# PSUM in eight tiles of one bank instead of four of two, reads of one bank each, and a new order of steps, in a fused attention and mixture-of-experts kernel

## The chip, the cores and the metric

The kernel runs on one core of a Trainium2 chip. The metric is the device time of one execution in microseconds; before the change it is 699.67 us, the median of three runs (698.33 to 700.05).

## What is computed

Linear attention feeds a mixture of four attention experts. Per batch (8) and head (8), with 576 positions and 64 channels:

```
phi(x) = concat(exp(p), exp(-p)),  p = x @ w_phi - max|x @ w_phi|        # 2 x 128 features
num = phi(q) @ (phi(k)^T v);  den = phi(q) @ sum(phi(k)) + 1e-6;  attn = num / den
```

The heads side by side give x (8 x 576 x 512). Each expert e projects x to q, k and v (512 to 64), takes causal softmax attention over the 576 positions and projects back to 512. The two experts with the largest gate logits (x @ w_gate) are kept per position, weighted with the softmax over their two logits, and added. The layout of inputs and outputs is prepared outside the timed program. All is in float32; the projections of x split each operand into a high and a low part (float32r) and take three products.

## The kernel before, in words

The work is cut into pairs of heads, 32 in all, p = 0 to 31, and into batches b = 0 to 7, each with two groups g of two experts. Generators describe the streams, and every `yield` is one step on one engine:

- `stream_k`: projects k of a pair on PE; `center` reduces its absolute maximum on DVE (L353) and subtracts it into the tile ek (L356); two exponentials follow on ACT. `stream_kv` multiplies by v and copies the result to kv.
- `stream_q`: projects q; `evac_u` copies the result out; `phi_q` takes the maximum over partitions on POOL (L438), subtracts on DVE (L447), and takes two exponentials on ACT. `stream_n` multiplies by kv, `divide` (with `normed`, L379 to L387) divides, `turn_x` transposes on PE (L393) and `evac_x` writes the high part xh and the low part xl.
- `stream_b`, per batch: `proj_t` projects q and k of a group in two pieces of 256 and 320 positions; `evac_q` and `evac_k` write high parts (qh on ACT at L171, kkh at L169 or L180) and low parts (ql at L522, kkl at L165) on DVE. `proj_v` projects v and the gate logits (vs; lg at L543). `scores` multiplies in four steps, `soft` adds the causal mask (L571), copies the scores to st, and keeps the running maximum in top (L588). `post` takes the maximum over partitions on POOL, subtracts (L673), exponentiates and multiplies with v on PE; `norm_y` divides, `turn_y` transposes, `evac_y` writes yh and yl, and `project_out` and `evac_o` make the output tile ot, which SP stores.

Every matmul writes to PSUM, which holds 128 partitions by eight banks of 512 floats. The kernel has four PSUM tiles of two banks each, all named ps_c in the profile. A step takes either one bank of a tile (`proj_t`, `proj_v`, `stream_kv`, the transpositions, `project_out`) or both (`stream_k`, `stream_q`, `stream_n`, `scores`, `post`); after the latter, one instruction on DVE or ACT reads both banks at once. The tile framework adds the semaphores, from which tile an instruction reads or writes.

The order of all steps is fixed in advance by the string PICKS: each pair of letters names the stream that moves on, and the bank that its step takes, or whether ACT or DVE does the copy. `take` hands out banks by their number, (tile, half):

```python
banks = [(i // 2, i % 2 + k) for k in range(st.n)]
keys = [('c', *x) for x in banks]
```

`in_order` then makes every engine keep the order in which the steps were recorded. `keep_warm` fills PE's first microseconds with small bf16 matmuls without a use.

Of the kernel before, what the change touches and what calls it, by code (L numbers as in the profile page):

```python
# [8 lines left out]
F32 = mybir.dt.float32  # L9
# [3 lines left out]
ALU = mybir.AluOpType  # L13
# [23 lines left out]
BANKS = 4  # L37
# [12 lines left out]
    "EACACACABABAAAAABAAAAAAAAAAAFCCAFEMADADAEGCAMAMAECNIFEBAAAPAAAOIAAAAAAFENIBAAAOAAANIAAAAFGFEEAOINAHAAAMIGAAAOAAAAACAAAEA"  # L50
    "ECEGBAMAPIJBHAQIGAPIOAMADAFEOIJAFCCAOAGIKGOAMIEAGACAEAEEPIOAMAECBAJBQIMAQIGAPIDAOGJAOHPAOIAAPAAAFEOIKCEAOINIOAEAMIEGNAOI"
    "JBDAMAPIMAEEGIJAFCMANICAMBAAPALALIMAJGOAPIAAGIMALIMIDAMIGAECMIDAFADEDAAAOINAIGGAOINIFACANIMHIAMCMAJEOIFIFANADANIMILIDAEA"
    "BAMIDCNAFAEGNALAMAOIMBPAIECAQAFINAMIKAMIEGHALIECGALAKIEEBAMALADAMAIGNIAAOIFIJAMIJAIAIAICFIBALIDAIDMAKADAJILENALFLIMAGACA"
    "NAFIJAMIMIJAKIDGJIGAFADEAAKIECJAHAMAMILIKIJAJIFAECBAEGJIKAEELAKAICLABAFIDAIDLIIGLAHHKILADAKIKIDAKIJAIIDEAAFGKIIALIKICAIA"
    "HAHHFIJIHGKAJIIIDAHCDAKIKIJIGAKIJIIAJIIAFDCAIIDEFIDGAAJIGAKIJIHCJIJIJIDAHDDAKIHAHEKIKIHGKILIHAMAKILAHCLAHAHGLIKAMILIMILA"
    "LIHHOAKIMALIHEOANIKAKIMIHFKILALIKAIEIAKALAKIIBIGKAHADCMAJIKAJIDEAAKIFAKIIICAKIEGIAIIFAECBALAJIKAGGLIJIIAKAIIJIIAIIDAEAII"
    "ECBAMAEEMAEAKIIABALAKCDANIKDIGIIMANAKALIIALILIIAHAKIJAHEHCMALIKEMILAKFMIFGCALIMIMALAMILIJIKADAFAKIDEAAKIHGJAGCJALIJIKIJI"
    "KAHAHAHAKIJIHBJINADAIIJADAHELILINAIALFMINILGHHLIMALIMAIALIIIHADCLIDAAAIAIIFELIIAKILICAIILIEGFAIAIIEEBALAGAIILAKIIALAMIKI"
    "IGMIKIDADAEELIDCMAFACAMIJILBFALELIJAHFLAMALIJAKIHGKAKIHHKAKIDCAAKAKIEAKIGELAMIKIKADABAHGDALIHHMAMIKIHAHAMAHCHEOIPAMIKANI"
    "HGOINAHAHCKALIHDMIPANILAMAMINIHAQAMILIMAMIHBQALAPILIMILAJANAMIJEJFMALIMAJGHADCNAKIKIKADAAAKIFHMIKILIKICAEEFAJIEABALAGGLA"  # L60
    "KIJAKAJIDAEEEABANALILIICJAIDJIMADANIIENIMAKIJANAIFNALELGMAJINAMAIHNADAKAJIDCAAKALIFFLIMIJANILACALIJGFAKIJIDAHEDAKIKIHAHC"
# [33 lines left out]
class Plan:  # L95
# [16 lines left out]
    def release(self, tag, t):  # L112
        self.free.add(t[0][1:])

    def take(self, st, i):
        banks = [(i // 2, i % 2 + k) for k in range(st.n)]
        assert all(x in self.free for x in banks)
        self.free -= set(banks)
        keys = [('c', *x) for x in banks]
        return (keys[0], self.both[i // 2][:, i % 2, :]) if st.n == 1 else (*keys, self.both[i // 2])  # L120

    def loop(self):
        for i, x in zip(PICKS[::2], PICKS[1::2]):
# [20 lines left out]
def tile_linear_attn_moe(ctx, tc, qt, kt, v, wts, out):  # L144
# [5 lines left out]
    plan.both = [pp.tile([128, 2, 512], F32, name=f"ps_c{i}") for i in range(BANKS)]  # L150
    plan.free = {(i, h) for i in range(BANKS) for h in range(2)}
    for t in plan.both:
        nc.vector.memset(t[:, :, NJ * V1 - 1:NJ * V1], 0.0)
# [171 lines left out]
    def stream_k():  # L325
        for p in range(NPAIRS):
            x, need = k_in[p % IB], [(f'k_in{p % IB}', n) for n in range(3)] + ['wphi']
            ready = lambda: ('load_k', p) in done and ('w', 0) in done
            for us in (slice(0, 8), slice(8, 9)):
                k0, k1, pp_ = yield Step('PE', need, 'c', ready, tiling=(64, 128), n=2)  # L330
                for n in range(4) if us.start == 0 else (4,):
                    for h, pk in enumerate((k0, k1)):
                        r = slice(64 * h, 64 * h + 64)
                        half_mm(pp_[:, h, 128 * (n % 4):128 * (n % 4) + 128], x[r, 128 * n:128 * n + 128], wf[r, 0:128], 128, pk, need)
                plan.spawn(center(p, us, (k0, k1), pp_))
            done.add(('proj_k', p))
            i = p % EKB
            ek, e0k, e1k = ek2[i], f'ek{i}0', f'ek{i}1'
            yield Step('ACT', [e1k], pred=lambda: all(('center', p, t) in done for t in (0, 8)))
            act(1152, ek[:, 0], ek[:, 1], [e0k], [e1k], AF.Exp)  # L340
            yield Step('ACT')
            act(1152, ek[:, 1], ek[:, 1], [e1k], [], AF.Exp, scale=-1.0)
            done.add(('phi_k', p))

    def center(p, us, pk, pp_):
        m, mk, e1 = pmax[p % 2], ('pmax', p % 2, us.start), ek2[p % EKB][:, 1, us, :]
        if us.start == 0:
            parts = [(slice(0, 128), 8, pp_.rearrange("p h (u f) -> p (h u) f", f=128))]
        else:
            parts = [(slice(64 * h, 64 * h + 64), 1, pp_[64 * h:64 * h + 64, h:h + 1, 0:128]) for h in range(2)]  # L350
        yield Step('DVE', list(pk), hot=True)
        for r, n, src in parts:
# [468 lines left out]
```

## Time and profile before

| | |
|---|---|
| median of 3 runs | 699.67 us |
| profiled execution | 699.21 us, span 697.4 us |
| busy: PE, DVE, ACT, POOL | 615.6, 508.4, 368.0, 200.6 us |
| mean granted TensorE clock | 0.977 |
| DMA | 43.45 MB, mean 62 GB/s |

How to read what follows: "L162" is a line of the kernel, "ps_c<-xh,qk" means that the instruction writes ps_c and reads xh and qk, "128x256" is partitions by elements per partition. "x6" counts instructions. In brackets stands the idle time of the engine ahead of an instruction, and what released it. PE is TensorE's matmuls, PEld its weight loads, DVE VectorE, ACT ScalarE, POOL GpSimd, SP the engine that issues DMAs.

### The profile page before, as it was taken

The page shows a single profiled execution, that of the slowest core. Times are in us where ns is not written, and L with a number is a line of the kernel's source. Part 1 is how long each engine was busy: PE and PEld are TensorE (multiplying, and loading weights), DVE is VectorE, ACT ScalarE, POOL GpSimd, SP SyncE. Part 2 cuts the span into 40 slices and gives each one's busy share as a digit, 9 for nine tenths or more (in the row PEclk, how much of TensorE's full clock was granted, in tenths as well). Part 3 has the DMA queues.
Part 4 walks back from the last instruction along what each step waited for, and adds up shares of the span by engine and source line. Part 5 has one row for each costly group of instructions (what it writes and reads, how often), then busy time and mean ns, then how long its engine had stood idle before and what let it go on. Part 6 is the DMA issues. An engine that isn't in the chain of part 4 may idle for free. (4 is left out here: it accounts for less than half of the span.)

```text
span 697.4 us, 22344 instructions
## 1 busy us (share of the span) xinstructions
PE 615.6 (88%) x9880; PEld 553.8 (79%) x9880; DVE 508.4 (73%) x1127; ACT 368.0 (53%) x561; POOL 200.6 (29%) x79
## 2 busy tenths in 40 slices
PE   8999998899888998988888888899988988987885
PEld 7888896888777897887778778788888777876774
DVE  6899788886696766898478767768576786555572
ACT  4988536566373544774146645454246455344442
POOL 5345306342242112542034332411060241120220
PEclk9999999999999999999999999899999999999999
DMA  7555213122131201423023031222112000010012
GB/s 199 130 152 153 63 39 90 40 58 56 39 108 37 75 20 38 127 74 75 3 70 91 19 82 31 57 72 75 30 46 90 18 22 0 3 53 18 1 53 85
DMA packets 60272, 43.45 MB, mean 62 GB/s; under 512 B 44688, under 2 KB 47248, under 8 KB 60176
## 3 DMA queue, kind: packets, MB, share of 16 engines
q1 hardware_dynamic: 60176, 42.03, 21.4%
q8 instruction: 77, 1.26, 0.7%
q14 instruction: 19, 0.16, 0.1%
HBM read 32.58 MB, written 9.44 MB: 60 GB/s over the span
## 5 line engine op out<-in xcount | busy, mean ns | idle before, releaser
L438 POOL PARTITION_ALL_REDUCE mx<-u x32 | 130.0, 4081 | 193.6 <-ACT u L169 193.5
L162 PE MATMUL ps_c<-xh,qk 128*128 128x320 f32 (+1 forms) x512 | 110.4, 302 | 10.2 <-DVE ql L522 6.5
L162 PEld LDWEIGHTS ps_c<-xh,qk 128*128 128x128 f32 x512 | 84.4, 190 | 14.3 <-DVE ql L522 7.8
L368 PE MATMUL ps_c<-v_in,ek 128*64 128x65 f32 x2560 | 87.6, 231 | 4.2 <-issue 0.9
L368 PEld LDWEIGHTS ps_c<-v_in,ek 128*64 128x64 f32 x2560 | 83.5, 146 | 8.4 <-DVE xl L165 1.3
L171 ACT ACTIVATE ek<-ek 128x1152 f32<-128x1152 f32 x64 | 74.6, 1166 | 22.8 <-DVE ek L356 22.3
L438 POOL PARTITION_ALL_REDUCE tops<-top x15 | 57.5, 3832 | 73.2 <-DVE top L588 73.2
L162 PE MATMUL ps_c<-xl,qk 128*128 128x256 f32 (+1 forms) x256 | 76.0, 297 | 0.0
L673 DVE TENSOR_TENSOR st<-st,tops 128x1152 f32<-128x1152 f32 (+4 forms) x75 | 68.8, 937 | 1.2 <-POOL tops L438 0.7
L171 ACT ACTIVATE st<-st 128x1152 f32<-128x1152 f32 (+3 forms) x60 | 51.4, 870 | 33.7 <-DVE st L673 32.7
L162 PE MATMUL ps_c<-vg,xh 128*128 128x260 f32 (+1 forms) x320 | 61.2, 290 | 8.2 <-DVE lg L543 5.0
L162 PE MATMUL ps_c<-yh,wo 128*128 128x256 f32 (+1 forms) x256 | 56.1, 311 | 13.5 <-ACT ot L169 3.7
L169 ACT COPY st<-ps_c 128x1024 f32<-128x1024 f32 (+1 forms) x58 | 47.2, 833 | 36.0 <-PE ps_c L560 17.8
L368 PE MATMUL ps_c<-kv,mx 128*64 128x65 f32 x1152 | 63.1, 227 | 2.9 <-ACT kv L169 1.9
L353 DVE TENSOR_REDUCE pmax<-ps_c 64x1 f32<-64x128 f32 (+1 forms) x96 | 56.3, 596 | 11.7 <-PE ps_c L323 10.3
L368 PE MATMUL ps_c<-kv,u 128*64 128x65 f32 x1152 | 60.2, 224 | 0.0
L356 DVE TENSOR_TENSOR ek<-ps_c,pmax 64x128 f32<-64x128 f32 (+1 forms) x96 | 56.3, 597 | 1.8
L162 PEld LDWEIGHTS ps_c<-vg,xh 128*128 128x128 f32 (+1 forms) x320 | 47.6, 178 | 11.6 <-DVE lg L543 6.7
L162 PEld LDWEIGHTS ps_c<-yh,wo 128*128 128x128 f32 x256 | 40.4, 189 | 20.2 <-ACT ot L169 5.6
L368 PEld LDWEIGHTS ps_c<-kv,mx 128*64 128x64 f32 x1152 | 48.2, 140 | 8.9 <-ACT kv L169 3.8
L447 DVE TENSOR_TENSOR u<-u,mx 128x1152 f32<-128x1152 f32 x32 | 54.4, 1702 | 1.1 <-POOL mx L438 0.7
L323 PE MATMUL ps_c<-wf,k_in 64*128 64x128 f32 x640 | 51.9, 299 | 2.5 <-DVE ek L356 1.0
(111 smaller groups left out, 1198.7 us busy)
## 6 DMA issues: line engine op xcount, KB each, us to landing
v_in<-in_v_dram SPq DMA_DIRECT2D x32, 320.0 KB, 3.6
q_in<-in_qt_dram SPq DMA_DIRECT2D x64, 144.0 KB, 2.9
out_dram<-ot SPq DMA_DIRECT2D x32, 288.0 KB, 2.1
k_in<-in_kt_dram SPq DMA_DIRECT2D x32, 160.0 KB, 3.0
k_in<-in_kt_dram SPq DMA_DIRECT2D x32, 128.0 KB, 3.0
ot<-in_wts_dram SPq DMA_DIRECT2D x5, 288.0 KB, 4.4
k_in<-in_kt_dram SPq DMA_DIRECT2D x32, 32.0 KB, 2.9
ot<-in_wts_dram SPq DMA_DIRECT2D x1, 232.0 KB, 3.9
```

Source lines behind the costliest of these rows:

```text
L162: nc.tensor.matmul(o, a, b, start=start, stop=stop, skip_group_check=True)
L169: nc.scalar.copy(o, i)
L171: nc.scalar.activation(o, i, func, **kw)
L323: nc.tensor.matmul(o, a, b, start=True, stop=True, skip_group_check=True)
L353: dve(n * 128, [mk], pk).tensor_reduce(out=m[r, us], in_=src, axis=AX.X, op=ALU.max, apply_absolute_value=True)
L356: dve(n * 128, [f'ek{p % EKB}1'], [*pk, mk]).tensor_tensor(out=e1[r], in0=src, in1=m[r, us].unsqueeze(2).to_broadcast([r.stop - r.start, n ...
L368: nc.tensor.matmul(o, a, b, start=start, stop=stop, skip_group_check=True)
L438: nc.gpsimd.partition_all_reduce(o, i, 128, op)
L447: dve(2 * S, [uk], [mk], port=True).tensor_tensor(out=U, in0=U, in1=M, op=ALU.subtract)
L673: dve(2 * n, [sj[j]], [*key, mk], port=True).tensor_tensor(out=a, in0=a, in1=tops[x][0:m, :, 128 * j:], op=ALU.subtract)
```

## The change

PSUM becomes eight tiles of one bank. A step that took both banks of a tile now takes any two free tiles, and what read two banks in one instruction becomes two instructions, each a step of its own with its own place in the order: `center`, `evac_u`, `soft` with masks, copies and running maxima, and `normed` with all its five or six instructions. POOL's copy of the first scores into top becomes a step `first_top`, which needs both copies to st. `post` tells the planner that its matmuls need only the first exponentials at the start; the framework's semaphores decide what it waits for. Some planner hints (`port=True`, a rate) change with no instruction of their own. PICKS is new from its first letter to its last; the matmuls of the computation are the same ones.

```diff
-BANKS = 4
+BANKS = 8
 PICKS = (
-    "EACACACABABAAAAABAAAAAAAAAAAFCCAFEMADADAEGCAMAMAECNIFEBAAAPAAAOIAAAAAAFENIBAAAOAAANIAAAAFGFEEAOINAHAAAMIGAAAOAAAAACAAAEA"
+    "AABABABABAAAAAAAAAAACAAAAAAAAABAAAERCAEjMIF1PIBAMIPAAAPAAAOIF9MIOAAAOANIAAMIAANAAADAAAEAFxMICAEANIFsNIAANANIAADAAAEAE6CAOI"
...
-    def take(self, st, i):
-        banks = [(i // 2, i % 2 + k) for k in range(st.n)]
+    def take(self, st, x):
+        banks = (x % 8,) if st.n == 1 else (x % 8, x // 8)
...
-    plan.both = [pp.tile([128, 2, 512], F32, name=f"ps_c{i}") for i in range(BANKS)]
-    plan.free = {(i, h) for i in range(BANKS) for h in range(2)}
+    plan.both = [pp.tile([128, 512], F32, name=f"ps_c{i}") for i in range(BANKS)]
+    plan.free = set(range(BANKS))
...
-                plan.spawn(center(p, us, (k0, k1), pp_))
+                for h, pk in enumerate((k0, k1)):
+                    plan.spawn(center(p, us, h, pk, pp_[h]))
...
-        for r, n, src in parts:
-            dve(n * 128, [mk], pk).tensor_reduce(out=m[r, us], in_=src, axis=AX.X, op=ALU.max, apply_absolute_value=True)
+        dve(n * 128, [mk], [pk]).tensor_reduce(out=m[r, us_], in_=src, axis=AX.X, op=ALU.max, apply_absolute_value=True)
...
-    def normed(pk, pp_, d, eps, o, w, extra=None):
+    def normed(n, pk, ps, d, eps, o, w, extra=None):
...
-        dve(512, [(w, 0)], [*pk, *dk]).tensor_tensor(out=o[:, 0:4, :].rearrange("p i (n x) -> p n i x", x=64), in0=blocks[:, :, 0:4, 0:64],
-                                                in1=d[:, :, 0:4].unsqueeze(3).to_broadcast([128, 2, 4, 64]), op=ALU.mult)
+        dve(256, [(w, 0, n)], [pk, *dk]).tensor_tensor(out=o[:, 0:4, r], in0=blocks[:, 0:4, 0:64],
+                                                       in1=d[:, 0:4].unsqueeze(2).to_broadcast([128, 4, 64]), op=ALU.mult)
...
-        copy(st_.eng, 2 * n, u[p % UB][:, :, s0:s1], pp_[:, :, 0:n], [f'u{p % UB}'], pk)
+        copy(st_.eng, n, u[p % UB][:, h, s0:s1], ps[:, 0:n], [('u', p % UB, s0, h)], [pk])
...
-                dve(2 * m, pk, []).tensor_tensor(out=pp_[0:m, :, o:o + m], in0=pp_[0:m, :, o:o + m],
-                                                 in1=mask[0:m, 0:m].unsqueeze(1).to_broadcast([m, 2, m]), op=ALU.add)
+                dve(m, [pk], []).tensor_tensor(out=ps[0:m, o:o + m], in0=ps[0:m, o:o + m], in1=mask[0:m, 0:m], op=ALU.add)
...
-        k0, k1, pp_ = yield Step('PE', ej, 'c', ready, tiling=(128, 64), n=2)
+        k0, k1, pp_ = yield Step('PE', ej[0:1], 'c', ready, tiling=(128, 64), n=3)
```

What moves is shown at three places. The number at the end of a tile's name tells its place in memory; ps_c0 to ps_c3 are tiles of two banks before, ps_c0 to ps_c7 tiles of one bank now.

ACT's queue in the last batch, second group, from the last copies of the first group's scores (st) over q's high parts (qh) to k's (kkh). Before:

```order
L169 COPY st1_143<-ps_c1_62 128x1024
L171 ACTIVATE qh_151<-ps_c2_63 128x256
L169 COPY st2_144<-ps_c0_61 128x1024
L171 ACTIVATE qh_151<-ps_c2_63 128x320
L169 CAST kkh_153<-ps_c2_63 128x256
L169 CAST kkh_153<-ps_c2_63 128x320
```

Now:

```order
L179 COPY st1_151<-ps_c4_65 128x512
L179 COPY st2_152<-ps_c0_61 128x512
L179 COPY st1_151<-ps_c6_67 128x512
L179 COPY st2_152<-ps_c5_66 128x512
L181 ACTIVATE qh_159<-ps_c2_63 128x256
L179 CAST yh1_181<-ps_c7_68 128x320
L179 CAST yh1_181<-ps_c3_64 128x256
L181 ACTIVATE qh_159<-ps_c1_62 128x320
L179 CAST kkh_161<-ps_c4_65 128x256
L179 CAST kkh_161<-ps_c6_67 128x320
```

The four pieces of q and k lay in the two banks of ps_c2; now each has a tile of its own, the copies of st are four instead of two, and a transposed y of the batch before (yh) is read in between.

PE's queue at the start of the last batch's output projection, its first two pieces (256 and 320 positions). Before:

```order
L162 MATMUL ps_c1_62<-yh0_171,wo_179 128x256 x2
L162 MATMUL ps_c1_62<-yl0_172,wo_179 128x256
L162 MATMUL ps_c1_62<-yh1_173,wo_179 128x256 x2
L162 MATMUL ps_c1_62<-yl1_174,wo_179 128x256
L162 MATMUL ps_c1_62<-yh0_171,wo_179 128x320 x2
L162 MATMUL ps_c1_62<-yl0_172,wo_179 128x320
```

Now:

```order
L172 MATMUL ps_c3_64<-yh0_179,wo_187 128x256 x2
L172 MATMUL ps_c3_64<-yl0_180,wo_187 128x256
L172 MATMUL ps_c3_64<-yh1_181,wo_187 128x256 x2
L172 MATMUL ps_c3_64<-yl1_182,wo_187 128x256
L172 MATMUL ps_c5_66<-yh0_179,wo_187 128x320 x2
L172 MATMUL ps_c5_66<-yl0_180,wo_187 128x320
```

Both pieces wrote the tile ps_c1, in its two banks, and so did the next four; now the eight pieces of this projection write eight tiles.

DVE's queue at the last division of the first group (sc is the divisor, gw the gate's weight, yq the result). Before:

```order
L379 TENSOR_SCALAR sc0_147<-ps_c1_62 128x10
L380 RECIPROCAL sc0_147<-sc0_147 128x10
L382 TENSOR_TENSOR sc0_147<-sc0_147,gw_170 128x10
L383 TENSOR_TENSOR yq0_149<-ps_c1_62,sc0_147 128x2x4x64
L387 TENSOR_SCALAR yq0_149<-ps_c1_62,sc0_147 64x64 x2
```

Now:

```order
L386 TENSOR_SCALAR sc0_155<-ps_c3_64 128x5
L387 RECIPROCAL sc0_155<-sc0_155 128x5
L389 TENSOR_TENSOR sc0_155<-sc0_155,gw_178 128x5
L390 TENSOR_TENSOR yq0_157<-ps_c3_64,sc0_155 128x4x64
L392 TENSOR_SCALAR yq0_157<-ps_c3_64,sc0_155 64x64
L386 TENSOR_SCALAR sc0_155<-ps_c5_66 128x5
L387 RECIPROCAL sc0_155<-sc0_155 128x5
L389 TENSOR_TENSOR sc0_155<-sc0_155,gw_178 128x5
L390 TENSOR_TENSOR yq0_157<-ps_c5_66,sc0_155 128x4x64
L392 TENSOR_SCALAR yq0_157<-ps_c5_66,sc0_155 64x64
```

Six instructions are ten, and the second five need only the second tile. Over the whole program DVE has 1,491 instructions instead of 1,128 and ACT 699 instead of 562; PE's warm-up matmuls are 129 instead of 72.

More of the change, by code (lines that the diff above doesn't have):

```diff
@@ L54 @@
[L54 to L61, printed above, removed]
@@ L336, in stream_k @@
             done.add(('proj_k', p))
             i = p % EKB
[L338 to L340 removed]
+            ek, e0k, e1k = ek2[i], f'ek{i}0', [(f'ek{i}1', t, h) for t in (0, 8) for h in range(2)]
+            yield Step('ACT', e1k, pred=lambda: all(('center', p, t, h) in done for t in (0, 8) for h in range(2)))
@@ L354, in center @@
+        src = ps[r, 0:128 * n].rearrange("p (u f) -> p u f", f=128)
+        yield Step('DVE', [pk], hot=True)
+        dve(n * 128, [mk], [pk]).tensor_reduce(out=m[r, us_], in_=src, axis=AX.X, op=ALU.max, apply_absolute_value=True)
         yield Step('DVE', [mk], pred=has('kv', p - EKB) if p >= EKB else None, hot=True)
-        for r, n, src in parts:
-            dve(n * 128, [f'ek{p % EKB}1'], [*pk, mk]).tensor_tensor(
-                out=e1[r], in0=src, in1=m[r, us].unsqueeze(2).to_broadcast([r.stop - r.start, n, 128]), op=ALU.subtract)
@@ L358, in center @@
-        free(pk)
-        done.add(('center', p, us.start))
+        dve(n * 128, [ek_k], [pk, mk]).tensor_tensor(
+            out=ek2[p % EKB][r, 1, us_, :], in0=src, in1=m[r, us_].unsqueeze(2).to_broadcast([r.stop - r.start, n, 128]), op=ALU.subtract)
+        plan.release('c', (pk, ps))
+        done.add(('center', p, us.start, h))
     def load_v():
@@ L443, in phi_q @@
         uk, mk = f'u{i}', f'mx{i}'
-        yield Step('POOL', [uk], pred=lambda: all(('u', p, s0) in done for s0, s1 in QPARTS))
-        reduce(2 * S, M, U, [mk], [uk], bass_isa.ReduceOp.absmax)
+        us = [('u', i, s0, h) for s0, s1 in QPARTS for h in range(2)]
+        yield Step('POOL', us, pred=lambda: all(('u', p, s0, h) in done for s0, s1 in QPARTS for h in range(2)))
+        reduce(2 * S, M, U, [mk], us, bass_isa.ReduceOp.absmax)
         yield Step('DVE', [mk])
@@ L563, in scores, with first_top @@
+                if n == 0:
+                    plan.spawn(first_top(g))
             done.add(('s', b, g))
             plan.spawn(post(b, g))
-        def soft(g, n, blocks, pk, pp_):
+        def first_top(g):
+            x = place(b, g)
+            sk = [('st', x, 0, e) for e in range(2)]
+            yield Step('POOL', sk, pred=lambda: all(('ev', b, g, 0, e) in done for e in range(2)))
+            nc.gpsimd.tensor_copy(top[x][:, :, 0:128], st[x][0][:, :, 0:128])
+            done.add(('tops', b, g, 0))
@@ L573, in soft @@
             x = place(b, g)
-            key, tk = [('st', x, k) for k in range(4)], [('top', x, k) for k in range(2)]
+            key, tk = [('st', x, k, e) for k in range(4)], ('top', x, 1, e)
             d_, c0 = AT[blocks[0][0]][0], 288 if n == 1 else 0
-            st_ = Step(copies(2 * w), list(pk), hot=True)
+            st_ = Step(copies(w), [pk], hot=True)
             yield st_
-            copy(st_.eng, 2 * w, st[x][d_][:, :, c0:c0 + w], pp_[:, :, 0:w], [key[n]], pk)
-            done.add(('ev', b, g, n))
@@ L580, in soft @@
-            if n == 0:
-                yield Step('POOL', [key[0]])
-                nc.gpsimd.tensor_copy(top[x][:, :, 0:128], st[x][0][:, :, 0:128])
-                done.add(('tops', b, g, 0))
+            copy(st_.eng, w, st[x][d_][:, e, c0:c0 + w], ps[:, 0:w], [key[n]], [pk])
+            done.add(('ev', b, g, n, e))
             for m, o, q0, q1 in TOPS[n]:
                 first = n == 2 and m == 128
-                yield Step('DVE', [*pk, key[0], key[1], tk[1]], hot=True,
-                           pred=(lambda: all(('ev', b, g, k) in done for k in (0, 1))) if first else has('tops', b, g, 1))
-                dve(2 * (q1 - q0), [tk[1]], [*pk, key[0], key[1]]).tensor_tensor(
-                    out=top[x][0:m, :, q0:q1], in0=pp_[0:m, :, o:o + q1 - q0],
-                    in1=(st[x][0] if first else top[x])[0:m, :, q0:q1], op=ALU.max)
-                done.add(('tops', b, g, 1))
@@ L592, in soft @@
-            free(pk)
-            done.add(('soft', b, g, n))
+                yield Step('DVE', [pk, key[0], key[1], tk], hot=True,
+                           pred=(lambda: all(('ev', b, g, k, e) in done for k in (0, 1))) if first else has('tops', b, g, 1, e))
+                dve(q1 - q0, [tk], [pk, key[0], key[1]]).tensor_tensor(
+                    out=top[x][0:m, e, q0:q1], in0=ps[0:m, o:o + q1 - q0],
+                    in1=(st[x][0] if first else top[x])[0:m, e, q0:q1], op=ALU.max)
+                done.add(('tops', b, g, 1, e))
```

202 lines of the change are left out of this document (112 added, 90 removed).

## The prediction

> **What bounds the kernel now.** First the page: who is busiest.
>
> ```profile
> span 697.4 us, 22344 instructions
> PE 615.6 (88%) x9880; PEld 553.8 (79%) x9880; DVE 508.4 (73%) x1127; ACT 368.0 (53%) x561; POOL 200.6 (29%) x79
> ```
>
> PE bounds it. It stands idle for 697.4 - 615.6 = 81.8 us; DVE is idle for 189 us and ACT for 329 us. So the question is what PE waits for, which the view of waits says for PE (engine, line, waited for: us in total, times, longest).
>
> ```profile
> PE ps_c L393 <- DVE kkl L165: 14.8, 9, 2.8
> PE ps_c L162 <- DVE ql L522: 7.6, 6, 2.6
> PE ps_c L162 <- DVE lg L543: 5.7, 9, 0.8
> PE ps_c L162 <- DVE yl L165: 4.8, 5, 1.3
> PE ps_c L162 <- ACT ot L169: 4.2, 9, 0.6
> PE ps_c L162 <- DVE xl L165: 3.6, 4, 1.1
> ...
> PE ps_c L393 <- ACT ot L169: 2.9, 4, 1.4
> PE ps_c L393 <- DVE ql L522: 2.5, 3, 1.1
> PE ps_c L162 <- DVE ot L180: 2.1, 4, 0.5
> ...
> PE ps_c L368 <- ACT st L171: 0.2, 1, 0.2
> ```
>
> All but the last row are one kind: PE waits until the reads of a step that owns a single bank (kkl, ql, lg, yl, xl, ot) are over. Their sum is 14.8 + 7.6 + 5.7 + 4.8 + 4.2 + 3.6 + 2.9 + 2.5 + 2.1 = 48.2 us. A transposition (L393) has no use for kkl as data, so this is a wait for room in PSUM, not for input. Softmax's long chain over POOL costs PE 0.2 us (last row).
>
> Why room is late is seen in the timeline, at the projections of the last batch's second group. It gives start, us, engine, line, what, and the idle time before; PE's rows first, then ACT's, then DVE's.
>
> ```profile
> 639.88 0.28 PE L162 MATMUL ps_c<-xl,qk 128*128 128x256 f32 x1
> 640.00 0.43 PE L162 MATMUL ps_c<-xh,qk 128*128 128x256 f32 x2
> 641.74 0.30 PE L162 MATMUL ps_c<-xh,qk 128*128 128x320 f32 x1
> 644.61 0.58 PE L162 MATMUL ps_c<-xh,qk 128*128 128x256 f32 x1 [2.57 <-DVE ql L522]
> 644.99 0.41 PE L162 MATMUL ps_c<-xl,qk 128*128 128x256 f32 x1
> ...
> 642.08 0.38 ACT L171 ACTIVATE qh<-ps_c 128x256 fp32r<-128x256 f32 x1 [2.10 <-PE ps_c L162]
> 642.36 1.01 ACT L169 COPY st<-ps_c 128x1024 f32<-128x1024 f32 x1
> 647.57 0.44 ACT L171 ACTIVATE qh<-ps_c 128x320 fp32r<-128x320 f32 x1 [4.21 <-PE ps_c L162]
> ...
> 643.40 0.82 DVE L588 TENSOR_TENSOR top<-ps_c,top 128x640 f32<-128x640 f32 x1 [1.78 <-ACT st L169]
> 644.14 0.41 DVE L522 SCALAR_TENSOR_TENSOR ql<-ps_c,qh 128x256 fp32r<-128x256 f32 x1
> ```
>
> PE writes the last of q's first part (256 columns) at 640.00 and goes straight on to the second part (320). ACT, idle for 2.10 us, starts the copy of the first part only at 642.08, when the second part's last matmul (641.74) is over. The two parts lie in the two banks of one tile, so a read of one bank waits for the write of its neighbour. Behind that copy queue ACT's copy of st, then DVE's maximum, then ql; and PE, which needs the first bank for k, stands still until 644.61. Then the game repeats: the second part's copy, whose data were there at 642.04, starts at 647.57. The planner hands out banks one by one (the key has the half in it), so it counted on none of these waits.
>
> **Part 1, a tile is one bank: waits that go.** A step with a single bank can no longer hold or be held by a neighbour, and all eight banks combine freely. I take all 48.2 us as gone: each of these rows is a write that waits for a read delayed in that way, or for the neighbour's read itself. Bounds: below, 24 us, if half are honest waits for a slow read; above, 56 us, since the view has some ten smaller rows of the same kind worth 8 us. What is late next: the reads themselves, behind DVE's queue (part 3).
>
> **Part 2, the clock.** The core's mean granted clock and two stretches behind that 2.57 us wait:
>
> ```profile
> core 0: 697.4 us, clock 0.977
> ...
> 644.00:648.00 4.00, 2.93 (x12) 2.63 (x12) 1.02 (x3) 0.43 (x1) 2.81 (x1) 0.57 0.00 0
> 648.00:652.00 4.00, 2.49 (x16) 2.19 (x16) 0.92 (x2) 0.38 (x2) 0.77 (x1) 1.00 0.00 0
> ```
>
> After the long wait the clock is 0.57, and the 256-column matmul takes 0.41 us (644.99) against 0.28 (639.88). Over the run the missing clock is 0.023 x 697.4 = 16 us. If the long waits go, so does most of it; I take 12, between 0 and 16. [...]
>
> **Part 3, every PSUM read is halved: what DVE and ACT pay.** Groups with their forms (busy us, mean ns of one), then four masks in a run:
>
> ```profile
> L353 DVE TENSOR_REDUCE pmax<-ps_c 128x8 f32<-128x1024 f32 x32 | 39.0, 1220 | 9.6 <-PE ps_c L323 9.2
> L353 DVE TENSOR_REDUCE pmax<-ps_c 64x1 f32<-64x128 f32 x64 | 18.2, 284 | 2.1 <-PE ps_c L323 1.1
> L571 DVE TENSOR_TENSOR ps_c<-ps_c,mask 128x256 f32<-128x256 f32 x64 | 26.1, 423 | 3.0 <-PE ps_c L560 2.5
> L379 DVE TENSOR_SCALAR rd<-ps_c 128x10 f32<-128x10 f32 x32 | 5.3, 164 | 7.7 <-PE ps_c L368 7.4
> L380 DVE RECIPROCAL rd<-rd 128x10 f32<-128x10 f32 x32 | 6.9, 217 | 1.1
> L382 DVE TENSOR_TENSOR sc<-sc,gw 128x10 f32<-128x10 f32 x16 | 4.3, 269 | 0.6
> L169 ACT COPY st<-ps_c 128x1024 f32<-128x1024 f32 x30 | 30.0, 1015 | 10.5 <-DVE ps_c L571 9.8 <-PE ps_c L560 0.5
> L169 ACT COPY st<-ps_c 128x576 f32<-128x576 f32 x28 | 17.4, 639 | 25.5 <-PE ps_c L560 17.3 <-DVE ps_c L571 5.0 <-issue 3.1
> ...
> 637.76 1.43 DVE L571 TENSOR_TENSOR ps_c<-ps_c,mask 128x256 f32<-128x256 f32 x4
> ```
>
> From 1220 ns for 1024 elements and 284 for 128, one element is 1.045 ns and the fixed part 150 ns, which each extra half pays again. The changed order has 64 more instructions in `center`, 80 more masks, 64 more maxima and 48 more divisions: 256 x 0.150 = 38 us. `normed` also doubles its small ones in 48 places, 16 of them with the gate: 48 x (0.164 + 0.217) + 16 x 0.269 = 22.6 us. Together 61 us. In a run they overlap: four masks take 1.43 us instead of 4 x 0.423 = 1.69, 0.087 less at each joint; over 368 instructions that is 32 us, so 29 is the lower end. I take 45, the middle: DVE goes to 553 us. What of it lies on the path depends on where DVE has no room:
>
> ```profile
> 25.00:50.00 25.00, 24.49 (x555) 21.17 (x553) 23.90 (x47) 21.25 (x32) 6.86 (x3) 1.00 0.51 134
> 50.00:75.00 25.00, 24.35 (x418) 21.08 (x414) 23.33 (x41) 19.70 (x28) 16.51 (x5) 1.00 0.46 123
> 100.00:125.00 25.00, 21.42 (x364) 17.61 (x362) 22.49 (x40) 15.47 (x26) 13.92 (x5) 1.00 0.24 63
> 275.00:300.00 25.00, 24.69 (x474) 22.28 (x473) 22.77 (x48) 18.54 (x28) 12.95 (x5) 1.00 0.37 106
> ...
> 675.00:697.40 22.40, 14.29 (x172) 12.26 (x170) 6.42 (x18) 4.98 (x12) 0.00 (x0) 0.96 0.21 80
> ```
>
> In each row the busy times follow the length: PE, PEld, DVE, ACT, POOL. The four rows ahead of the dots are those with DVE near 22.5 us of 25 or over; they hold 92.5 of its 508.4 us, 18%. There extra work adds to the time, elsewhere PE's work covers it: 0.18 x 45 = 8 us. Ends: 0, and all 61. ACT runs 137 more instructions of (1015 - 448 x 0.839 = 639 at 576 elements, so) 0.156 us fixed each, 21 us, under its 329 us of idle time: nothing. If that cover were gone, 21.
>
> **Part 4, the order.** The start now has 129 warm-up matmuls instead of 72, and each costs
>
> ```profile
> 9.70 1.01 PE L162 MATMUL ps_c<-warm 128*128 128x128 bf16 x15
> ```
>
> 1.01 / 15 = 0.067 us; 57 more are 3.8 us. They may fill time in which PE waits for DVE's halves anyway (then 0); I take 4. SP now loads k ahead of q at the start: at most about a microsecond either way, taken as 0. POOL's copy of st into top now waits for two ACT copies in place of one; behind it in POOL's queue stands the all-reduce that needs that same copy, and POOL is idle 71% of the time: 0. Elsewhere the order moves whole steps; each bank is given out again later in PE's queue, and I credit nothing beyond part 1.
>
> **Sum**, against the profiled execution: 697.4 - 48.2 - 12 + 8 + 4 = 649.2 us of span; that run took 699.2 in all, 1.8 more than its span, so **651 us**. Its 699.2 and the median 699.67 differ by less than the 0.3% (2 us) that a measurement can tell from no change.
>
> **Rivals.**
> Nearer to PE's floor. In 25:75 PE is 97.7% busy with DVE at 94%, because those steps take both banks of a tile and meet no neighbour. If all of the run came to look so: (615.6 - 12 + 4) / 0.977 = 622, plus the 8.1 us that PE idles in the last 22.4, plus 1.8: 632 us. Against it: DVE's extra work. Chance 0.10.
>
> DVE's queue takes over part of the waits. At 553 of 649 us DVE would be 85% busy and serves in order; reads of a bank then queue behind halves of other steps. If half of the 48.2 us returns: 651 + 24 = 675. For it: the wait at 644.61 had DVE's maximum ahead of ql. Against it: halves leave DVE earlier for the next read. Chance 0.17.
>
> Slower. DVE's 27% of idle time may come from chains of data (reduce, subtract, exponential) and not from neighbours; then the share stays and the time follows DVE's work: 553 / 0.729 = 759, plus 1.8: 760 us. It decides where DVE cannot pass 553 / 697 = 79% busy. Against it: 25:75, at 94%. [...] Chance 0.05.
>
> No change: the waits at PSUM only hide another chain of the same length, and the time stays within 0.3%, 697.6 to 701.8. The 0.2 us for the exponentials speak against it. Chance 0.03.
>
> **The numbers.** My forecast, 651, has 0.65 and a range of its own from 638 to 664. The 80% range takes in most of the first two rivals, 628 to 682. It leaves out slower (0.05), no change (0.03) and the tails of the other two. Faster by over 0.3%: 0.65 + 0.10 + 0.17 = 0.92; within 0.3% 0.03; slower 0.05.
>
> **What would show it.** In the profile after: PE's waits for kkl, ql, lg, yl, xl and ot together under 15 us; copies qh and kkh starting within 0.3 us of the end of their own part's matmuls when ACT is free; the clock at 0.99 or more; DVE's busy time between 537 and 569; PE at about 94%. I am wrong if these waits persist with the same length, if DVE's busy time passes 570, or if PE waits longer for ek, xq or yq than now.

## The result, and the profile after

The changed kernel takes 614.36 us (median of 4 runs, 613.67 to 614.85); the kernel before, beside it, 699.86 us. The ratio is 0.878, with a 95% interval from 0.875 to 0.880. The forecast of 651 us had the direction right and the gain too small by 37 us, outside its range of 628 to 682. One of the runs below, of the new order with four tiles, was slow: 818.84 us at a clock of 0.929, where the other three of its kernel took 801.07 to 811.76 us at 0.943 to 0.956.

The head of the page, of the kernel after:

```profile
span 612.2 us, 23048 instructions
PE 592.6 (97%) x9937; PEld 547.9 (89%) x9937; DVE 538.0 (88%) x1490; ACT 379.6 (62%) x698; POOL 198.8 (32%) x79
```

The span is 85.2 us shorter. PE's idle time went from 81.8 to 612.2 - 592.6 = 19.6 us, which is 62.2; and PE's busy time fell by 23.0 us, though it issues 57 matmuls more. DVE works 29.6 us longer than before. What PE still waits for (engine, line, waited for: us, times, longest; the rows of 1 us and over):

```profile
PE ps_c L398 <- DVE yq L390: 2.8, 3, 2.4
PE ps_c L374 <- ACT kv L179: 2.0, 1, 2.0
PE ps_c L568 <- DVE lg L551: 2.0, 1, 2.0
PE ps_c L374 <- ACT st L181: 1.8, 3, 0.7
PE ps_c L329 <- DMA q_in<-in_qt_dram: 1.6, 2, 1.2
PE ps_c L172 <- DVE col L203: 1.3, 1, 1.3
PE ps_c L398 <- DVE xq L390: 1.1, 2, 0.8
```

Of the waits for kkl, ql, lg, yl, xl and ot, whose largest rows made up the 48.2 us, only one for lg (2.0 us, now ahead of the scores, L568) is left. The timeline at the same place as before, the projections of the last batch's second group; PE, then ACT, then DVE:

```profile
567.96 0.28 PE L172 MATMUL ps_c<-xh,qk 128*128 128x256 f32 x1
568.07 0.80 PE L398 MATMUL ps_c<-ident,yq 128*128 128x128 f32 x5
568.81 0.41 PE L172 MATMUL ps_c<-xh,qk 128*128 128x320 f32 x1
...
571.99 0.42 PE L172 MATMUL ps_c<-xh,qk 128*128 128x256 f32 x2
572.25 0.31 PE L172 MATMUL ps_c<-xl,qk 128*128 128x320 f32 x1
...
573.72 0.31 PE L172 MATMUL ps_c<-xh,qk 128*128 128x320 f32 x1
...
567.65 2.05 ACT L179 COPY st<-ps_c 128x512 f32<-128x512 f32 x4 [1.24 <-DVE ps_c L588]
569.57 0.43 ACT L181 ACTIVATE qh<-ps_c 128x256 fp32r<-128x256 f32 x1
570.88 0.44 ACT L181 ACTIVATE qh<-ps_c 128x320 fp32r<-128x320 f32 x1 [0.29 <-PE ps_c L172]
572.31 0.37 ACT L179 CAST kkh<-ps_c 128x256 fp32r<-128x256 f32 x1 [0.99 <-PE ps_c L172]
574.10 0.43 ACT L179 CAST kkh<-ps_c 128x320 fp32r<-128x320 f32 x1 [1.43 <-PE ps_c L172]
...
570.05 0.41 DVE L530 SCALAR_TENSOR_TENSOR ql<-ps_c,qh 128x256 fp32r<-128x256 f32 x1
```

The row at 571.99 holds the last matmul of k's first part and the first of the second part; the former, 0.28 us long, is over at about 572.27, and the copy kkh of that part starts at 572.31, while PE writes the second part until 574.03 (573.72 + 0.31). The copy no longer waits until its neighbour is written; that of the second part follows at 574.10. The first qh waits only for ACT's own copies of st. Where PE stood still for 2.57 us before, it has no gap in brackets. The core's clock:

```profile
core 0: 612.2 us, clock 0.994
```

And two of the halved groups of DVE (busy us, mean ns of one):

```profile
L360 DVE TENSOR_REDUCE pmax<-ps_c 128x4 f32<-128x512 f32 x64 | 42.8, 682 | 6.6 <-PE ps_c L329 6.0
L588 DVE TENSOR_TENSOR ps_c<-ps_c,mask 128x128 f32<-128x128 f32 x128 | 32.3, 287 | 1.3 <-PE ps_c L568 1.1
```

Two halves of 682 ns stand for one of 1220: 0.144 us more, about the fixed part of 0.150 that the prediction had worked out; and two masks of 287 ns for one of 423: 0.151 us more.

### The profile page after: what moved, and what is told of

Same layout as the page of the kernel before. It is cut to its first block, busy times and chain, and to the rows that moved or that the text cites. A ratio compares the mean times of both kernels' runs of the same rounds, so it can differ in the third digit from the quotient of the medians.

```text
span 612.2 us, 23048 instructions
## 1 busy us (share of the span) xinstructions
PE 592.6 (97%) x9937; PEld 547.9 (89%) x9937; DVE 538.0 (88%) x1490; ACT 379.6 (62%) x698; POOL 198.8 (32%) x79
## 4 chain that ended last, share of the span: by engine, by line
PE 49%; DVE 35%; ACT 6%; issue 3%; DMA 3%; POOL 3%; SPq 1%; ACTq 0%; DVEq 0%; POOLq 0%
PE ps_c L172 21%; PE ps_c L374 14%; PE ps_c L329 7%; DVE ek L362 4%; DVE pmax L360 4%; PE ps_c L568 4%; DVE st L685 4%; DVE u L454 3%; PE ps_c L398 3%; DVE top L600 3%; ACT ek L181 2%; POOL mx L444 2%; DMA q_in<-in_qt_dram 2%; DVE ps_c L588 2%; DVE xq L390 1%
## 5 line engine op out<-in xcount | busy, mean ns | idle before, releaser
L172 PE MATMUL ps_c<-xh,qk 128*128 128x320 f32 (+1 forms) x512 | 106.6, 299 | 0.8 <-DVE top L600 0.4
L444 POOL PARTITION_ALL_REDUCE tops<-top x15 | 53.8, 3584 | 94.1 <-DVE top L600 52.2
L374 PE MATMUL ps_c<-v_in,ek 128*64 128x65 f32 x2560 | 81.6, 222 | 0.7 <-ACT u L179 0.3
L374 PEld LDWEIGHTS ps_c<-v_in,ek 128*64 128x64 f32 x2560 | 77.5, 137 | 5.1 <-issue 1.3
L685 DVE TENSOR_TENSOR st<-st,tops 128x1152 f32<-128x1152 f32 (+4 forms) x75 | 64.5, 881 | 1.6 <-POOL tops L444 1.2
L179 ACT COPY st<-ps_c 128x288 f32<-128x288 f32 (+1 forms) x105 | 47.1, 497 | 23.4 <-DVE ps_c L588 16.7
L362 DVE TENSOR_TENSOR ek<-ps_c,pmax 128x512 f32<-128x512 f32 (+1 forms) x128 | 59.6, 483 | 2.0
L581 POOL COPY top<-st 128x256 f32<-128x256 f32 x15 | 6.1, 405 | 143.6 <-ACT st L179 125.8
L179 ACT COPY u<-ps_c 128x288 f32<-128x288 f32 (+1 forms) x122 | 41.8, 412 | 14.7 <-PE ps_c L329 14.1
L374 PEld LDWEIGHTS ps_c<-vs,st 128*64 128x64 f32 x1500 | 45.4, 138 | 5.0 <-ACT st L181 2.5
```

The source lines that it names most:

```text
L172: nc.tensor.matmul(o, a, b, start=start, stop=stop, skip_group_check=True)
L179: nc.scalar.copy(o, i)
L362: dve(n * 128, [ek_k], [pk, mk]).tensor_tensor(out=ek2[p % EKB][r, 1, us_, :], in0=src, in1=m[r, us_].unsqueeze(2).to_broadcast([r.stop - ...
L374: nc.tensor.matmul(o, a, b, start=start, stop=stop, skip_group_check=True)
L444: nc.gpsimd.partition_all_reduce(o, i, 128, op)
L685: dve(2 * n, [sj[j]], [*key, mk], port=True).tensor_tensor(out=a, in0=a, in1=tops[x][0:m, :, 128 * j:], op=ALU.subtract)
```

## Tiles, halves and order, one at a time

The change does three things at once. Two theories stood against each other: that the tiles end the waits and the order adds nothing (the forecast's), or that the order brings a part of its own. The first runs keep the old order and split each read of two banks in place. Ratios are to the kernel before, run beside each on the same chip. There it took 696 to 701 us, so times of runs on different chips compare to some 4 us.

**Old order, four tiles, halves alone.** The edit to every such read, here the copy of u:

```diff
-        copy(st_.eng, 2 * n, u[p % UB][:, :, s0:s1], pp_[:, :, 0:n], [f'u{p % UB}'], pk)
+        for h in range(2):
+            copy(st_.eng, n, u[p % UB][:, h, s0:s1], pp_[h][:, 0:n], [f'u{p % UB}'], pk)
```

> The kernel before with its own order and its four tiles of two banks; alone every step that read both banks in one instruction now issues one for each bank, in the same step. Theory (the pairing of two banks in a tile makes the waits): those waits stay, DVE's busy time rises from 508 to about 538 us, and the time does not fall: 695 to 715 us. Rival (shorter reads by themselves, which let the next read start earlier, made the gain): under 670 us.

Measured: 739.53 us against 697.2 for the kernel before on the same chip, ratio 1.064 (1.057 to 1.071). The halves cost 42 us, against the theory's 18 at most. Its page:

```profile
span 738.4 us, 22875 instructions
PE 629.2 (85%) x9880; PEld 565.5 (77%) x9880; DVE 552.4 (75%) x1500; ACT 376.6 (51%) x684; POOL 197.8 (27%) x79
```

Its first waits of PE:

```profile
PE ps_c L397 <- DVE kkl L168: 18.3, 9, 3.0
PE ps_c L397 <- DVE xq L389: 11.8, 9, 2.9
PE ps_c L165 <- DVE ql L527: 8.4, 6, 3.4
```

The same row for xq in the kernel before, whose rows for kkl and ql stand in the prediction:

```profile
PE ps_c L393 <- DVE xq L383: 1.9, 3, 0.9
```

The waits for kkl and ql are somewhat longer than before (14.8 and 7.6 there), and transpositions now wait 11.8 us for xq instead of 1.9: DVE is done with the division later than the order had assumed. Of the 41 us of span, 27.4 are idle time of PE (81.8 to 109.2) and 13.6 its longer busy time, in which the lower clock (0.955, where it was 0.977) shows.

**Old order, eight tiles.** The same kernel, with each bank a tile:

```diff
-        return self.both[x[0]][:, x[1], :]
+        return self.both[2 * x[0] + x[1]]
...
-    plan.both = [pp.tile([128, 2, 512], F32, name=f"ps_c{i}") for i in range(BANKS)]
+    plan.both = [pp.tile([128, 512], F32, name=f"ps_c{i}") for i in range(2 * BANKS)]
```

> The kernel before with its own order, halved reads as in the run beside it, and each bank a tile of its own. Nothing else moves. Theory of the prediction (the tiles alone end the waits for the neighbour; the order adds nothing): 620 us or less, near the changed kernel's 614, since the order has nothing left to add. Rival (the tiles bring about what the prediction summed up, and the new order, made for eight free banks and for halves, brings the rest): 640 to 665 us, with PE idle for 35 to 50 us where the changed kernel has 20. If over 690, the tiles alone are worth nothing.

Measured: 650.23 us, ratio 0.935 (0.929 to 0.940), so 89 us less than with four tiles. The second theory holds. Its page:

```profile
span 649.4 us, 22923 instructions
PE 607.4 (94%) x9880; PEld 553.9 (85%) x9880; DVE 543.4 (84%) x1504; ACT 377.0 (58%) x684; POOL 198.2 (31%) x79
```

Its first waits of PE:

```profile
PE ps_c L397 <- DVE xq L389: 6.8, 8, 2.4
PE ps_c L397 <- DVE kkl L168: 4.8, 5, 1.5
PE ps_c L397 <- DVE yq L389: 4.6, 5, 2.8
PE ps_c L397 <- ACT ot L172: 2.5, 1, 2.5
PE ps_c L165 <- DVE lg L548: 2.0, 2, 1.2
PE ps_c L165 <- DVE ql L527: 1.8, 2, 1.5
```

PE idles for 649.4 - 607.4 = 42.0 us. The same order with halves and four tiles had 738.4 - 629.2 = 109.2 us. All rows for kkl, ql, lg, yl, xl and ot together came to 59.9 us there (53.8 in the kernel before) and come to 13.7 us here, so the tiles alone end most of these waits. In the lead is now xq, with kkl and yq behind.

**New order, four tiles.** The changed kernel with its banks as halves of tiles:

```diff
-    plan.both = [pp.tile([128, 512], F32, name=f"ps_c{i}") for i in range(BANKS)]
+    two = [pp.tile([128, 2, 512], F32, name=f"ps_c{i}") for i in range(BANKS // 2)]
+    plan.both = [two[i // 2][:, i % 2, :] for i in range(BANKS)]
```

> The changed kernel with its new order and its halved reads, but with banks 0 and 1, 2 and 3, 4 and 5, 6 and 7 as halves of one tile each. Theory (pairing makes the waits): they come back, and in greater number than before, because the new order pairs and reuses banks freely: 690 to 760 us, PE's idle time at 80 us or more, and again waits of PE for kkl, ql, yl, xl and ot. Rival (the order made the gain): within 10 us of 614.

Measured: 809.2 us (801.07 to 818.84; 806.63 without the longest), ratio 1.159 (1.150 to 1.168), beyond even the theory's 760. So the order's worth depends on the tiles: with four it costs 67 to 70 us against the 739.5 of the old one, with eight it brings 650.2 - 614.0 = 36. The first waits are not those that I had named, kkl, ql, yl, xl and ot, but for steps that own two banks (profile of the run of 818.84 us):

```profile
PE ps_c L173 <- DVE top L601: 8.6, 7, 2.0
PE ps_c L375 <- DVE ek L363: 6.8, 5, 2.1
PE ps_c L173 <- DVE xq L393: 6.5, 2, 5.3
```

**Fewer warm-up matmuls.**

```diff
-            for _ in range(3):
+            turns += 1
+            for _ in range(3 if turns <= 24 else 0):
```

> The changed kernel with 72 of its 129 warm-up matmuls; the last 57 of them are left out. The prediction's part 4 priced them at 4 us: then about 610.5 us. Rival (they fill time in which PE has nothing to do before the first halves come back, or hold the clock up): 613 to 616 us, no change.

Measured: 613.99 us, ratio 0.882 (0.877 to 0.886), not to be told from the changed kernel's 0.878. The rival holds: the 57 matmuls cost nothing that can be told, and not the 4 us. That they hold the clock up was not shown: without them its mean is 0.991 to 0.997, with them 0.993 or 0.994.

| order | four tiles, whole reads | four tiles, halves | eight tiles, halves |
|---|---|---|---|
| old | 697.2 | 739.5 | 650.2 |
| new | | 809.2 | 614.0 to 614.4 |

## What in the order brings 36 us

Two guesses from the waits of the old order with eight tiles: transpositions come too soon behind their division, and banks are given out in fixed pairs. Both were tried in that kernel, by a new string of picks with otherwise the same steps. `take` accepts any two banks there, as in the changed kernel; of the string, the second line with transpositions put back:

```diff
-    "ECEGBAMAPIJBHAQIGAPIOAMADAFEOIJAFCCAOAGIKGOAMIEAGACAEAEEPIOAMAECBAJBQIMAQIGAPIDAOGJAOHPAOIAAPAAAFEOIKCEAOINIOAEAMIEGNAOI"
+    "EaE-BAMAPIJBHAQIGAPIOAMADAFsOIJAFaCAOAGIK-OAMIEAGACAEAEsPIOAMAEaBAJBQIMAQIGAPIDAJAPIAAOGAAFsOHOAKaQAOIEANIOAEAMIExNAPIJE"
...
```

> The old order with eight tiles (650.2 us), in which a transposition of xq or yq that came less than 5.5 us of PE work behind the product that it divides is put back until it does, with the reads of its result: 23 of 48, by 2.1 us on average. 5.5 us is about the lower quartile of the new order; in the old one it is 3.6 and 2.6. Theory A (the new order gains by giving the division more time ahead of the transposition): the 11.4 us in which transpositions wait for xq and yq go, with some 4 us of stops: 634 to 640 us. Rival B (it gains by other things: when and which banks come free, halves as steps of their own): 646 to 654 us.

Measured: 659.63 us, ratio 0.947 (0.944 to 0.951): slower than the 0.935 it started from, and beyond the range of rival B too. Theory A falls. Its first waits:

```profile
PE ps_c L163 <- DVE xq L389: 6.8, 3, 4.6
PE ps_c L395 <- DVE kkl L166: 4.7, 5, 1.5
PE ps_c L324 <- DVE xl L166: 3.6, 4, 1.1
```

The transpositions wait less for xq, but projections (L163) now wait for the bank that the division still reads (6.8 us), and others (L324) for xl (3.6 us), which is read later too.

And with every step in its place but another bank, the first line:

```diff
-    "EACACACABABAAAAABAAAAAAAAAAAFCCAFEMADADAEGCAMAMAECNIFEBAAAPAAAOIAAAAAAFENIBAAAOAAANIAAAAFGFEEAOINAHAAAMIGAAAOAAAAACAAAEA"
+    "EACACACABABAAAAABAAAAAAAAAAAFRCAFjMADADAE1CAMAMAEXNIFhBAAAPAAAOIAAAAAAFjNIBAAAOAAANIAAAAFpFmEAOINAHAAAMIGAAAOAAAAACAAAEA"
...
```

> The old order with eight tiles and every step where it was; only which bank a step gets is changed: always the one that has been free longest, two of them for a step with two, whichever they are. Theory (the old table was bound to pairs of neighbours, and the new one gains by taking any bank): the 13 us of PE's waits for kkl, ot, ql and lg go, and the time is 635 to 642 us. Rival (the banks were far enough apart once each has a tile of its own): 647 to 653 us.

Measured: 648.14 us, ratio 0.928 (0.922 to 0.934). Its interval meets that of the start (0.929 to 0.940): at most a few us, and not the 36. The rival holds.

> Both edits of the two runs beside it in one kernel. If they are what the new order gains: 614 to 625 us. If the gain lies in the halves as steps of their own, or is spread over the whole order: 640 us or more.

Measured: 649.73 us, ratio 0.933 (0.930 to 0.936). No gain; the choice of banks only makes good what the later transpositions had cost.

**Halves joined again.** In the changed kernel the two halves of a read are steps of their own, with 2.5 to 3.5 other steps of DVE between them on average in `center` and 1.5 to 2.5 in `divide`, counted in the trace. Two kernels take the changed string and move one half to the other; its first line for the later place and for the earlier one (the lines with a minus are the changed kernel's; the line with a plus under "The change" has two letters, "EA", more than the kernel):

```diff
-    "AABABABABAAAAAAAAAAACAAAAAAAAABAAAERCAEjMIF1PIBAMIPAAAPAAAOIF9MIOAAAOANIAAMIAANAAADAAAFxMICAEANIFsNIAANANIAADAAAEAE6CAOI"
+    "AABABABABAAAAAAAAAAACAAAAAAAAABAAAERCAEjF1BAAAQAQAAAF9MINIAAQAQAOIPIAAMIMIAAOAAADAAAFxMIMICAEAFsNINIAANANIAADAAAEAE6CAEZ"
...
```

```diff
-    "AABABABABAAAAAAAAAAACAAAAAAAAABAAAERCAEjMIF1PIBAMIPAAAPAAAOIF9MIOAAAOANIAAMIAANAAADAAAFxMICAEANIFsNIAANANIAADAAAEAE6CAOI"
+    "AABABABABAAAAAAAAAAACAAAAAAAAABAAAERCAEjMINIF1OIPIBAMIMIOAOAAAAAMIMIF9MAMAAAAAAAMAAADAAAFxCAEANINIFsAANANIAADAAAEAE6CAOI"
...
```

> The changed kernel (614 us), in which the reads of the two halves of a step with two banks, which it had made steps of their own, stand next to each other again, both at the place of the later one, so that the first bank comes free with the second. PE's order stays but for some 30 steps that must come later, and about 125 steps get another bank. Theory (halves as steps of their own make the order's gain): 635 to 655 us. Rival (the places of the halves don't matter): 612 to 622 us.

Measured: 671.52 us, ratio 0.964 (0.961 to 0.968), beyond the theory's 655. Some of it can belong to the 30 steps of PE and the 125 banks that had to change with it.

> The changed kernel, in which the reads of the two halves of a step with two banks stand next to each other, both at the place of the earlier one (in the run before they stood at the place of the later one, 671.5 us). All banks and PE's order are as in the changed kernel. If those 57 us came from reading the first half late: 612 to 625 us. If the gain of the order is that other steps stand between the halves: 640 us or more.

Measured: 642.76 us, ratio 0.923 (0.914 to 0.932). At the later place the halves cost 57 us, at the earlier one 28. The 643 us fall into the second range (640 us or more), yet half of the 57 us do come from the later place. So it seems that both ends matter: the first bank should be read early, and the second read should not stand ahead of what is more urgent. The reason for the second is a reading, not a run of its own.

**DVE's work.** The halves had added 35 us of DVE's work (543.4 - 508.4) to an order that was laid out without it. Taking about as much away (the mask) in both orders:

```diff
-                dve(m, [pk], []).tensor_tensor(out=ps[0:m, o:o + m], in0=ps[0:m, o:o + m], in1=mask[0:m, 0:m], op=ALU.add)
```

> The old order with eight tiles (650.2 us) without the addition of the causal mask: 160 instructions and some 36 us of DVE's work are left out, so the weights of later positions are not taken away. That brings DVE back to about the 508 us for which the old order was laid out. Theory C (the old order has stretches without room on DVE, and the halves' extra 35 us fall there): most of the order's 36 us come back, 615 to 630 us. Rival D (DVE is not the cause; the places of the steps are): 643 us or more.

Measured: 636.48 us, ratio 0.914 (0.904 to 0.923): 14 us less for 29.3 us less on DVE (514.1 busy), between the two theories.

> The changed kernel (614.4 us) without the addition of the causal mask, as in the run beside it. Theory C: the new order hides DVE's work already, so the same 36 us less of it bring little, 606 to 614 us. If DVE still sets part of the time at 88% busy: under 600 us.

Measured: 612.33 us, ratio 0.879 (0.871 to 0.887): nothing that can be told. Then more work in the new order, first the same line a second time, in all 160 places:

> The changed kernel with every addition of the mask made twice: 160 instructions and about 36 us of work more on DVE, which comes to about 574 us. What the prediction's rival of DVE's queue speaks of, in the new order. Theory C (the new order has used up the room, it has no slack for unplanned work): 630 to 650 us, as the old order paid for its halves. Rival (PE's work covers it, DVE has 12% of idle time): 614 to 622 us.

Measured: 660.62 us, ratio 0.949 (0.941 to 0.958), beyond theory C's 650. Its page:

```profile
span 661.2 us, 23203 instructions
PE 611.5 (92%) x9937; PEld 558.9 (85%) x9937; DVE 583.3 (88%) x1650; ACT 378.6 (57%) x698; POOL 199.1 (30%) x79
```

DVE's busy time rose by 583.3 - 538.0 = 45.3 us, the time by 46 (50 by the ratios), at a DVE that is idle for 12% of the span before and after. That the two agree is in part chance: of the 49.0 us of span between the profiles, 30.1 are idle time of PE (19.6 to 49.7) and 18.9 its longer busy time, some 12 of them by the clock (0.976, where it was 0.994). Then the line for one half only (`if e == 0`), and the same number of instructions on ACT:

```diff
+                nc.scalar.copy(spare[0:m, 0:m], mask[0:m, 0:m])
```

> The changed kernel with the addition of the mask made twice for one of the two halves only: 80 instructions more on DVE, about 22 us. Theory E1 (from 88% on, DVE's work counts in full): half of the 46 us of the run with all 160, 634 to 640 us. Rival (the first 20 us are still covered by DVE's idle time and only the rest counts): 614 to 624 us.

Measured: 634.81 us, ratio 0.908 (0.900 to 0.916): 20 us for 22 us more on DVE (560.2 busy). That is in E1's range.

> The changed kernel with a copy of the mask to a spare place in SBUF on ACT behind each of its 160 additions of the mask: about 36 us more for ACT, which was busy for 380 of 612 us, in a place that the order had not planned for. Theory E (DVE is what has no room at 88%; ACT has it): 614 to 622 us. Rival F (the order is laid out so closely that unplanned work on any engine costs more than its length, as it did on DVE: 46 us for 45): 640 us or more.

Measured: 627.62 us, ratio 0.898 (0.892 to 0.904): 13 us for 33 us more on ACT (412.5 busy), between the two theories. So neither engine takes unplanned work for nothing; the doubled masks count about in full, ACT's copies for less than half. The two differ in more than the engine, though: the second mask stands in the chain from the scores to their copy st and keeps a bank occupied for longer, while nothing waits for ACT's copy but ACT itself. Whether DVE's lack of room or this place sets the higher price isn't told apart; a run with as much work on DVE outside such a chain is missing.

How the new order places DVE's work is seen in stretches of 25 us in which DVE is nearly full, at 23 us and more. Three of nine in the old order with eight tiles, then three of thirteen in the changed kernel (PE, PEld, DVE, ACT and POOL busy, as in the prediction):

```profile
300.00:325.00 25.00, 21.97 (x481) 20.19 (x479) 24.06 (x58) 15.79 (x22) 4.45 (x1) 1.00 0.30 79
350.00:375.00 25.00, 22.02 (x431) 19.35 (x428) 23.32 (x57) 17.71 (x33) 12.22 (x4) 1.00 0.34 101
525.00:550.00 25.00, 21.52 (x361) 19.03 (x360) 23.18 (x54) 15.97 (x29) 12.34 (x3) 1.00 0.10 27
```

```profile
50.00:75.00 25.00, 25.00 (x477) 22.88 (x473) 24.34 (x51) 17.46 (x29) 8.89 (x2) 1.00 0.45 121
300.00:325.00 25.00, 24.17 (x398) 21.81 (x399) 24.43 (x53) 19.19 (x33) 16.12 (x5) 1.00 0.35 89
375.00:400.00 25.00, 25.00 (x330) 23.95 (x327) 23.76 (x68) 16.40 (x27) 9.66 (x4) 1.00 0.13 37
```

In the nine of the old order PE gets 21.5 to 24.1 us, 22.7 on average; in the thirteen of the new one 24.2 to 25.0, 24.7 on average. Without the mask the two orders are 24 us apart (636.48 and 612.33, on one chip) instead of 36. So some 12 of the 36 us hang on the mask: on the work that it gives DVE or on its place in the chain to st, which these runs leave out together. The rest was not tied to one move: the places of the halves count (28 and 57 us when they are joined), putting back transpositions and choosing other banks in the old order bring nothing. Which other moves of the new order matter stays open.

## Why the prediction was wrong

Its terms, against what the two profiles show (us of span; the split of PE's busy time is an estimate from the mean clocks):

| step | predicted | measured |
|---|---|---|
| waits for reads of one-bank steps | -48.2 | -46.2 (2.0 for lg are left) |
| all other waits of PE | 0 | -16.0 (the rest of 62.2) |
| clock | -12 | -12.3 (0.023 x 697.4 = 16.0 to 0.006 x 612.2 = 3.7) |
| PE's busy time beside the clock | +4 | -10.7 (the rest of 23.0) |
| halves on DVE | +8 | none seen beside the rows above |
| sum | -48.2 | -85.2 |

**The step that failed** is part 4's "Elsewhere the order moves whole steps; each bank is given out again later in PE's queue, and I credit nothing beyond part 1." The order brought 36 us, nearly the whole miss of 37. Between the profiles (649.4 and 612.2 us) that is 22.4 us of PE's idle time (42.0 to 19.6) and 14.8 of its busy time. Without the order, and without part 4's 4 us for warm-up matmuls, which the old order lacks, the forecast would have been 647, and 650.2 were measured. That is partly luck, since two of its prices were off against each other: by the runs, halves in the old order cost 42 us rather than 8, and the tiles bring 89 rather than 48.2 + 12.

**Part 3** failed in a way that goes with it. The 18% came from the stretches of the old order, and were taken over to an order of which I knew only that it was new. DVE's extra was 29.6 us, at the lower end of 29 to 61, where I took the middle; the rows of halves had the lengths foretold, but they follow each other closely. In the old order with four tiles it cost about all of itself (42 us for 44.0 on DVE); in the new one none is seen. Both are near the ends that I had allowed (0 and 61), neither near my 8 us.

**Part 1** held: tiles make the waits (739.5 us with four and 650.2 with eight, with the same instructions in the same order), and kkl, ql, yl, xl and ot left the view. The copies kkh start 0.04 and 0.07 us after their own part's end. But the tiles alone left 13.7 us of these waits, besides those for xq and yq that the halves had brought; they went with the order.

**Part 2** held in size: 12.3 us between the two profiles. That is luck in part, as the kernel before, over its runs beside these kernels, has a mean clock of 0.971 to 0.991, and takes 704 us at 0.971 and 691 at 0.991; against its best runs the term would have been some 2.5 us (0.009 x 689.5 = 6.2 to 3.7). The changed kernel has 0.993 or 0.994 in all four. PE's waits in the view of before are 2.8 us at most, and three quarters of the missing clock (12.3 of 16.0 us) went when they did. In the trace of before the granted clock is 0.50 in nine stretches and 1.00 elsewhere; seven of the nine are 3.41 us long. The 0.57 of the prediction's row comes from such a stretch, here with the one ahead of it (columns as there, PE's busy time first, the clock third from the end):

```profile
640.79:644.20 3.41, 1.25 (x9) 0.99 (x7) 1.63 (x5) 1.29 (x2) 0.00 (x0) 1.00 0.00 0
644.20:647.61 3.41, 2.93 (x12) 2.63 (x12) 0.82 (x3) 0.04 (x1) 2.42 (x1) 0.50 0.00 0
```

The stretch ahead is not idle as a whole: PE works for 1.25 of its 3.41 us. Counted in the trace of before, PE idled for 50 to 72% of the 3.41 us ahead of each of the nine, and for at most 47% of any other such stretch. This is a reading of that one trace and no tested rule; I did not find it as clear in the other runs.

**Part 4's** 4 us for warm-up came to 0 by the run with 72.

PE's busy time has a part that none of my terms had. In the timeline of before, matmuls of 320 columns start 0.15 us apart, but the last one ahead of a stop counts with its full 0.30:

```profile
641.59 0.31 PE L162 MATMUL ps_c<-xl,qk 128*128 128x320 f32 x1
641.74 0.30 PE L162 MATMUL ps_c<-xh,qk 128*128 128x320 f32 x1
```

PE had 101 gaps of 50 ns and more between matmuls before, 59 in the old order with eight tiles, and has 25 now, counted in the traces. 76 x 0.15 = 11.4 us are most of what went: the 10.7 of the table, and 3.8 more that the added warm-up matmuls hide. Other runs of the changed order bear the sign out, with some 0.2 us for a gap: beside the clock, PE's busy time is 588.9 us with 25 gaps, 592.4 with 43 (ACT's copies) and 595.6 with 62 (masks twice). The old order with eight tiles doesn't fit, with 42 gaps fewer and only some 3 us less. This is read off, not tested by a run of its own.

**Rivals.** "Nearer PE's floor" (632, chance 0.10) described best what came: PE at 97%, with DVE near 24 of 25 us in places. It was given too little because I held DVE's extra work against it, and its price was too high by the 15 us that PE's busy time fell below the 607.6 assumed there. "DVE's queue" did take over waits (xq and yq), but in the old order. "Slower" fell: DVE passes 79% busy and reaches 88%. Yet its thought, that DVE can't fill all its time, may be true from there on: the doubled masks count about in full. All the signs that I had named came out as foretold but for PE's share; they tested parts 1 to 3, and the order had none.

## What to carry to other kernels

An order that is laid out in advance is worth something only together with the durations and the buffers for which it was made: the same order cost 67 to 70 us with four tiles and brought 36 with eight, and masks of 45 us added to it cost 46. When a change brings a new plan along with a mechanism, price the plan as a term of its own, between nothing and the bottleneck's idle time that the mechanism leaves, rather than at zero. And idle time of an engine is not room: ask in which stretches it lies, and whether the plan knew of the work.

## What the runs showed that I had not expected

Splitting reads and nothing else cost 42 us with DVE at only 73% (508.4 of 697.4) beforehand, while its own busy time grew by 44.0 us (552.4): the idle quarter hid next to none of it. In the new order, with DVE at 88%, doubled masks cost about 1 us for each us added (20 for 22, 46 for 45), and work on ACT at 62%, for which nobody waits, still costs 13 for 33.
